# Causal triangle by matmul in the first two blocks, a new queue model in the planner, and a new order of the whole kernel

## The chip, the cores and the metric

The kernel runs on one core of one Trainium2 chip. A core has five engines with a queue each, which take their instructions strictly in the order in which the program gives them: TensorE (PE, matmuls; its weight loads are listed as PEld), VectorE (DVE), ScalarE (ACT), GpSimd (POOL) and SyncE (SP). DMA transfers are issued from two of them: from SP, whose descriptors the hardware makes, and from POOL, where software makes them; a transfer from POOL can convert f32 to bf16 on its way. Both kinds run on the same 16 DMA engines. The metric is the device time of one execution in microseconds; less is better.

## What is computed

The reference is causal attention with a choice of key chunks, followed by a two-layer network with a softplus between the layers. Cut to what matters:

```python
# q, k, v: (4, 8, 768, 64) f32; w_in: (512, 2048), w_out: (2048, 512)
k_min, k_max = k_chunks.min(3), k_chunks.max(3)          # chunks of 32 keys
ub = sum(maximum(q * k_min, q * k_max), axis=-1)          # bound per query and chunk
ub = where(causal, ub, -1e9)
top_chunks = argsort(ub)[..., -6:]                        # 6 chunks per query
scores = q @ k.T / 8
scores = where(selected & (pos_q >= pos_k), scores, -1e9)
attn = softmax(scores)
x = attn @ v                                              # (3072, 512)
h = x @ w_in
out = softplus(h) @ w_out                                 # f32
```

## The kernel before

The 3072 rows are 12 blocks of 256 queries: 4 batches with 3 blocks each. For each block n the kernel loads k, q and v, prepares them (k and q turned so that the head dimension lies on the partitions, the minima and maxima of the key chunks, the positive and negative part of q), computes the bounds with matmuls ("ub"), finds the sixth largest with DVE, and writes the resulting mask as extra rows below q, so that the score matmul adds the mask itself. These extra rows meet rows of ones and zeros per chunk (`ohb`, made by POOL and copied by SP into `KA` and `KB`, names "ohk"). For each of the 4 pairs of heads follow the scores ("s", lines 687 and 688), the exponential on ACT ("ex", line 695), the product with v ("av", line 717), the division by the sum ("nm", lines 727 and 728, into a buffer of the pool `osb`), and the turning of the result into `x`: by PE ("oT", line 743) in blocks 0 to 2 and 11, by a DMA transpose from SP ("xD") in the others. Then come the layers: "h" (line 791: 8 groups of 8 matmuls per block), two exponentials ("e", line 796) and a logarithm ("ln", line 801), and "y" (line 816), copied out and stored.

In the block on the diagonal, keys after the query must not count. Inside a 128 by 128 tile this triangle is cut out by POOL, after the exponential, with an affine select on `pt` ("af", line 705), and the product with v waits for it.

The first loads differ from the later ones. k and q of block 0 are loaded as f32 by SP (`load_pairs`, line 352) into `xp` and cast by ACT; everything else is loaded and cast by POOL (`load`, line 339; weights at 376 and 383). k and q are turned by PE in blocks 0 to 2 (line 471), by DMA transposes from block 3 on.

The order of the instructions is not written by hand. `make_plan` lists operations with a cost per engine, with what they need, and with a due time; `Plan.run` places them one after the other on a model of the engines and of two DMA queues, and takes the operation that is due first among those that can start soonest (within a tolerance `tol` per engine). Buffers come from pools whose sizes stand in `PAR["sizes"]`. The due times come from `PAR` (`a`, `prep`, `hlag` and others). `keep_awake` (line 852) then puts matmuls of zeros into the gaps that the plan leaves on PE in the first 45 us. The result is a fixed order on each engine; on the chip an instruction waits only for what it needs and for what stands ahead of it in its queue. In particular `rel`, the earliest time of an operation, is read only here:

```python
    def data_at(self, o, e):
        if e not in o.at:
            t = o.rel
            for d in o.deps + o.gate:
```

Block 3's loads and some copies on SP have a real dependency on the last piece of w_out (`gate`).

## Time and profile before

| | us |
|---|---|
| median of 3 runs | 267.46 (266.27 to 268.2) |
| the profiled execution | 266.59 |
| its span, first to last instruction | 264.8 |
| zero matmuls on PE (line 852), 243 of them | 22.7 |
| selects of the triangle on POOL (line 705), 96 of them | 39.5 |
| granted clock of TensorE, mean | 0.994 |

Busy time of an engine is what its instructions took; the page gives it as a share of the span. In the lists of instructions a row has the start and the time in us, the engine, the line, the operation, output and inputs, the count of like instructions in a row, and in square brackets how long the engine had been idle before and what ended that. "SPq" and "POOL ... DMA" rows are the issue of a transfer, not the transfer itself. Views by stage give the length of the stage, busy time and count (x) of each engine, the granted clock, the mean number of DMA packets at work per DMA engine, and GB/s.

### The profile page before, as it was taken

What the parts mean: (1) busy time and instruction counts of PE and PEld (TensorE: products, weight loads), DVE (VectorE), ACT (ScalarE), POOL (GpSimd) and SP (SyncE); (2) the same over time, 40 slices, a digit from 0 to 9 for tenths busy, and PEclk for the clock granted to TensorE, in tenths of its full rate; (3) what the DMA queues carried; (4) which work ended last, traced back from release to release, by engine and by line L of the source; (5) the groups of instructions that cost most, each with busy time, mean ns of one, the idle gap of its engine ahead of it and who ended that gap; (6) DMA issues with size and microseconds to landing.
All of it is one profiled execution on the core that took longest, in us unless ns stands there. A gap on an engine that the chain in (4) does not pass through costs nothing.

```text
span 264.8 us, 7039 instructions
## 1 busy us (share of the span) xinstructions
PE 255.0 (96%) x2750; PEld 197.2 (74%) x2779; DVE 142.5 (54%) x500; ACT 211.0 (80%) x372; POOL 110.8 (42%) x193
## 2 busy tenths in 40 slices
PE   8698999999999999999999999999999999999995
PEld 8698898768775677788678864777888756887744
DVE  6589961019789667447634596584582164221012
ACT  3589999988687879999687992699997885999900
POOL 8927878798318520543990263401110211310000
PEclk9799999999999999999999999999999999999999
DMA  7996999999999984699699969624440123001022
GB/s 162 161 189 90 181 196 231 155 139 190 149 136 173 132 119 89 115 129 100 73 173 150 117 88 174 173 54 120 45 82 0 42 72 99 10 2 42 0 79 79
DMA packets 114719, 29.87 MB, mean 113 GB/s; under 512 B 104544, under 2 KB 111712, under 8 KB 114688
## 3 DMA queue, kind: packets, MB, share of 16 engines
q0 software_dynamic: 74944, 13.11, 66.5%
q1 hardware_dynamic: 39744, 16.33, 33.0%
q8 instruction: 21, 0.34, 0.6%
q14 instruction: 10, 0.08, 0.1%
HBM read 27.26 MB, written 6.29 MB: 127 GB/s over the span
## 4 chain that ended last, share of the span: by engine, by line
PE 86%; DMA 5%; DVE 3%; ACT 3%; issue 1%; POOL 0%; DVEq 0%; POOLq 0%
PE ph L791 30%; PE py L816 17%; PE pt L816 9%; PE po L717 7%; PE ps L687 5%; PE py L852 4%; PE ps L688 4%; DMA io<-in_k_dram 3%; DMA x<-osb 3%; PE pt L687 2%; PE pt L688 1%; PE pt L570 1%; ACT g L801 1%; PE ph L816 1%; ACT e L796 1%
## 5 line engine op out<-in xcount | busy, mean ns | idle before, releaser
L791 PE MATMUL ph<-x,w_in_sb 128*128 128x256 bf16 x768 | 91.8, 272 | 0.0
L705 POOL TENSOR_SCALAR_AFFINE_SELECT pt<-pt 128x256 bf16<-128x256 bf16 x96 | 39.5, 419 | 112.6 <-ACT pt L695 112.1
L791 PEld LDWEIGHTS <-w_in_sb 128*128 128x128 bf16 x768 | 73.6, 98 | 11.5 <-DMA w_in_sb<-in_moe_w_in_dram 0.5
L695 ACT ACTIVATE pt<-ps 128x512 bf16<-128x512 f32 (+1 forms) x134 | 69.9, 564 | 9.4 <-PE ps L688 8.8
L796 ACT ACTIVATE e<-ph 128x512 f32<-128x512 f32 x96 | 56.3, 606 | 12.5 <-PE ph L791 11.8
L816 PEld LDWEIGHTS <-g 128*128 128x128 bf16 x400 | 37.4, 98 | 31.4 <-ACT g L801 0.5
L816 PE MATMUL py<-w_out_sb,g 128*128 128x512 bf16 x231 | 57.8, 379 | 1.5 <-ACT ysb L258 0.2
L801 ACT ACTIVATE g<-e 128x1024 bf16<-128x1024 f32 x48 | 51.1, 1072 | 1.0
L695 ACT ACTIVATE pt<-pt 128x512 bf16<-128x512 f32 (+1 forms) x58 | 32.4, 584 | 0.6 <-PE pt L688 0.6
L717 PEld LDWEIGHTS <-pt 128*128 128x128 bf16 x672 | 26.8, 97 | 5.1 <-issue 0.6
L259 DVE COPY ysb<-py 128x512 f32<-128x512 f32 x12 | 8.3, 691 | 36.9 <-PE py L816 36.9
L717 PE MATMUL po<-v,pt 128*128 128x65 bf16 x610 | 26.4, 193 | 0.3 <-DVE osb L728 0.3
L816 PE MATMUL pt<-w_out_sb,g 128*128 128x512 bf16 x108 | 26.2, 379 | 0.2
L727 DVE RECIPROCAL rec<-po 128x4 f32<-128x4 f32 x43 | 7.6, 178 | 34.9 <-PE po L717 34.6
L490 DVE TENSOR_REDUCE kx<-kT 128x32 bf16<-128x1024 bf16 x18 | 21.0, 1209 | 8.9 <-DMA kT<-io 8.9
L852 PE MATMUL py<-zero 128*128 128x128 bf16 x243 | 22.7, 245 | 1.1 <-DVE zero L268 1.1
L339 POOL DMA_DIRECT2D v<-in_v_dram x24 | 21.6, 905 | 3.8 <-DMA io<-in_q_dram 1.5
L339 POOL DMA_DIRECT2D io<-in_k_dram x22 | 20.0, 910 | 5.7 <-DMA w_in_sb<-in_moe_w_in_dram 2.2
L339 POOL DMA_DIRECT2D io<-in_q_dram x22 | 19.9, 910 | 0.7 <-PE ph L791 0.6
L728 DVE TENSOR_TENSOR osb<-po,rec 128x256 bf16<-128x256 f32 x43 | 18.2, 424 | 2.7 <-DMA x<-osb 1.3
L852 PEld LDWEIGHTS <-zero 128*128 128x128 bf16 x243 | 18.3, 111 | 1.3 <-DVE zero L268 1.1
L687 PE MATMUL ps<-qa,ka 96*128 96x256 bf16 x71 | 18.3, 273 | 0.7 <-DVE qa L259 0.7
(99 smaller groups left out, 302.5 us busy)
## 6 DMA issues: line engine op xcount, KB each, us to landing
out_dram<-ysb SPq DMA_DIRECT2D x23, 256.0 KB, 2.4
v<-in_v_dram POOLq DMA_DIRECT2D x24, 128.0 KB, 7.6
io<-in_k_dram POOLq DMA_DIRECT2D x22, 128.0 KB, 7.2
io<-in_q_dram POOLq DMA_DIRECT2D x22, 128.0 KB, 7.1
w_out_sb<-in_moe_w_out_dram POOLq DMA_DIRECT2D x4, 512.0 KB, 8.0
w_in_sb<-in_moe_w_in_dram POOLq DMA_DIRECT2D x4, 512.0 KB, 9.6
xp<-in_k_dram SPq DMA_DIRECT2D x2, 256.0 KB, 3.2
xp<-in_q_dram SPq DMA_DIRECT2D x2, 256.0 KB, 6.3
```

What stands on the lines that cost most here:

```text
L339: lambda e, t=t: nc.gpsimd.dma_start(out=into(nm, n, t), in_=rows(nm, n, t)),
L490: nc.vector.tensor_reduce(kx.ap[:, :, j].rearrange("d p (t c) -> d t p c", t=NT), kT.ap.rearrange("d p x -> d (p x)").rearrange("d (t p c ...
L687: nc.tensor.matmul(sp.ap[:, 0:QB], kk[0:nr, p, j * 128:(j + 1) * 128], qq, start=True, stop=True)
L695: lambda e, sp=sp, pt=pt, h=h, j=j, w=w: nc.scalar.activation(pt.ap[:, h, j:j + 2].rearrange("k j c -> k (j c)")[:, 0:w], sp.ap[:, 0:w], A ...
L705: nc.gpsimd.affine_select(out=d, in_=d, compare_op=ALU.is_ge, fill=0.0, base=0, channel_multiplier=-1, pattern=[[0, 2], [1, 128]])
L717: nc.tensor.matmul(o[:, u, h], pt.ap[:, h, j, c0:c0 + 128], T.V[i][:, j, 2 * p + h, :], start=(j == 0), stop=(j == t0 + u))
L728: nc.vector.tensor_tensor(osb.ap[0], o[:, :, :, 0:D], osb.ap[1].to_broadcast([128, NT, 2, D]), op=ALU.mult)
L791: nc.tensor.matmul(o[:, j], T.w_in[:, dt, ft * 128:(ft + 1) * 128], x.ap[:, dt], start=(dt == 0), stop=(dt == KDM - 1))
L796: lambda e, hb=hb, eb=eb, f2=f2: nc.scalar.activation(eb.ap[:, f2 * 512:(f2 + 1) * 512], hb.ap, ACT.Exp),
L801: lambda e, eb=eb, g=g, f4=f4: nc.scalar.activation(g.ap[:, f4 * 4:(f4 + 1) * 4].rearrange("f j c -> f (j c)"), eb.ap, ACT.Ln, bias=1.0),
L816: nc.tensor.matmul(yb.ap[:, 0:c1 - c0], g.ap[:, f, u * 128:(u + 1) * 128], T.w_out[:, f, c0:c1], start=(f == 0), stop=(f == KFF - 1))
L852: z.fn = lambda e: T.nc.tensor.matmul(T.pools["y"].homes[0][:, 0:128], T.zero, T.zero, start=True, stop=True)
```

## The change

The triangle of blocks 0 and 1 (`tri=2`) is no longer selected by POOL. Two more matmuls per last score group add a tile `T.tri` (0 where the key counts, -240000 where it doesn't) through the identity, before the exponential; the 16 selects of these blocks go. The zero matmuls may be 512 columns wide. The planner gets a new model of the two DMA queues (`Rings`): packets alternate between the two, a transfer that starts late is held back, at most 7 software transfers are out at once, and landing times change by kind (`land`, `packet`, `pen`). The software loads of blocks 0 to 2 get `rel=3300`. All due times are new, a table `tweak` adds an offset to the due time of about 170 names of operations, `tol` of POOL goes from 2358 to 9819 and of ACT from 0 to 150, `alt` (the handicap of an operation's second engine) from 636 to 48. The pools io, osb and e shrink from 8, 4 and 4 buffers to 6, 3 and 2. Options `both` and `l0 >= 3` are added and not used.

```diff
+class Rings:
+    def __init__(self):
+        self.t, self.q, self.on = 0.0, {"POOL": [], "SP": []}, {"POOL": False, "SP": False}
+        self.slots = []
...
+    def add(self, o, now):
+        self.run(max(now, self.t), [])
+        e = "POOL" if o.eng == "POOL" else "SP"
+        if e == "POOL":
+            if len(self.slots) >= 7:
+                o.end = max(o.end, self.slots[-7].done - self.slots[-7].land + 200)
+            self.slots.append(o)
...
+        for o in topo:
+            o.due += 1e3 * par["tweak"].get(o.name, 0.0)
...
-    tol={"PE": 0, "ACT": 0, "DVE": 0, "POOL": 2358, "SP": 0},
-    alt=636,
-    a=(-46.8, -33.92, -31.03, -0.05, 17.1, 24.77, 54.71, 88.7, 133.12, 175.62, 173.66, 255.42, 297.45, 469.8),
-    sizes=dict(s=2, h=2, y=1, o=1, t=2, xf=2, xp=4, kT=2, io=8, kx=2, q=2, pn=2, ub=2, pt=4, osb=4, x=4, g=2, e=4, ysb=4, mT=2),
+    tol={"PE": 0, "ACT": 150, "DVE": 0, "POOL": 9819, "SP": 0},
+    alt=48,
+    a=(-73.83, -47.43, -47.0, -44.3, 27.28, 71.21, 103.27, 111.52, 147.33, 256.72, 285.03, 350.27, 490.15, 633.52),
+    sizes=dict(s=2, h=2, y=1, o=1, t=2, xf=2, xp=4, kT=2, io=6, kx=2, q=2, pn=2, ub=2, pt=4, osb=3, x=4, g=2, e=2, ysb=4, mT=2),
...
+    tri_ = []
+    if par["tri"]:
+        t0_ = P.op("tri0", [("DVE", 100)], lambda e: nc.vector.memset(T.tri, 0.0), key=2000)
+        tri_ = [P.op("tri", [("POOL", 430)], lambda e: nc.gpsimd.affine_select(
+            out=T.tri, in_=T.tri, compare_op=ALU.is_ge, fill=NEG, base=0, channel_multiplier=-1, pattern=[[1, 128]]), [t0_], key=8000), ident]
...
-                     gate=gate, key=key, rel=key - 2000 if n > 2 else 0.0, dma=950 if n < 3 else 2050, packet=32.0, **new)
+                     gate=gate, key=key, rel=key - 2000 if n > 2 else 3300.0 if par["l0"] == 1 else 0.0, dma=850, packet=13.3, land=SKEW if n < 4 else 900.0, **new)
...
-                        nc.tensor.matmul(sp.ap[:, 0:QB], kk[0:nr, p, j * 128:(j + 1) * 128], qq, start=True, stop=True)
-                        nc.tensor.matmul(sp.ap[:, QB:w], kk[0:nr, p, (j + 1) * 128:(j + 2) * 128],
-                                         qq[:, 1] if last else qq, start=True, stop=True)
+                        add = last and tri
+                        for c0, c1, x in ((0, QB, qq), (QB, w, qq[:, 1] if last else qq)):
+                            jj = j + c0 // QB
+                            nc.tensor.matmul(sp.ap[:, c0:c1], kk[0:nr, p, jj * 128:(jj + 1) * 128], x, start=True, stop=not add)
+                            if add:
+                                nc.tensor.matmul(sp.ap[:, c0:c0 + 128], T.ident, T.tri, start=False, stop=True)
...
-                    if last:
+                    if last and not tri:
...
-        while True:
-            c = 107 if t < 1e3 * par["awake"][2] else mm(128)
...
+        for w in (512, 128):
+            while True:
+                c = w / 1.2 if t < 1e3 * par["awake"][2] else mm(w)
...
-    T.zero = sb.tile([128, 128], BF16, name="zero")
+    T.zero = sb.tile([128, 512], BF16, name="zero")
+    T.tri = sb.tile([128, 128], BF16, name="tri")
```

In `tweak` the names at issue below read `"w_out1": 70.83`, `"w_out0": -10.19`, `"w_in0": -1.54`, `"w_in1": 8.48`, `"oh": 19.6`, `"tri": -1.15`; the pieces of w_in and of w_out keep their order among themselves.

More of the change, by code (lines that the diff above doesn't have):

```diff
@@ L65 @@
 class Op:
     __slots__ = ("name", "alts", "fn", "deps", "gate", "after", "succ", "alloc", "touch", "key",
-                 "rel", "packet", "port", "due", "wait", "eng", "start", "end", "done", "dma", "n", "at", "inst")
+                 "rel", "packet", "port", "land", "pen", "due", "wait", "eng", "start", "end", "done", "dma", "n", "at", "inst")
 class Plan:
@@ L837, in keep_awake @@
 def keep_awake(T, order, par):
-    fill, free = [], 1e3 * par["awake"][0]
+    fill, free = [], max(1e3 * par["awake"][0], 140 + next(o.end for o in order if o.name == "zero"))
     for o in order:
```

204 lines of the change are left out of this document (141 added, 63 removed).

## The prediction

> **What bounds the kernel now.** I read the page first, then the busy time of each engine by stage, then the zero matmuls of line 852 by the same stages, and last the timeline of the first 44 us.
>
> ```profile
> span 264.8 us, 7039 instructions
> PE 255.0 (96%) x2750; PEld 197.2 (74%) x2779; DVE 142.5 (54%) x500; ACT 211.0 (80%) x372; POOL 110.8 (42%) x193
> ```
>
> PE is busy 96% of the span and no other engine is above 80%. But a part of PE's time is filler, so the average must be split into stages.
>
> ```profile
> core 0: us, PE busy (x) PEld busy (x) DVE busy (x) ACT busy (x) POOL busy (x), PEclk, DMA share, GB/s
> 0.00:18.00 18.00, 14.69 (x187) 14.13 (x188) 12.10 (x38) 10.22 (x15) 14.30 (x28) 0.91 1.57 167
> 18.00:28.00 10.00, 9.21 (x161) 8.43 (x160) 9.54 (x35) 9.47 (x16) 6.56 (x13) 1.00 0.86 123
> 28.00:36.00 8.00, 7.58 (x131) 6.68 (x129) 7.50 (x34) 7.78 (x17) 6.46 (x13) 1.00 1.34 184
> 36.00:44.00 8.00, 8.00 (x103) 7.27 (x102) 2.59 (x10) 7.35 (x15) 6.80 (x11) 1.00 1.22 220
> 44.00:261.20 217.20, 215.19 (x2175) 160.65 (x2202) 109.88 (x383) 176.17 (x312) 76.65 (x131) 1.00 0.95 102
> 261.20:264.80 3.60, 0.34 (x4) 0.06 (x1) 0.85 (x2) 0.00 (x0) 0.00 (x0) 1.00 0.21 73
> ```
>
> The zero matmuls alone, in the same stages:
>
> ```profile
> 0.00:18.00 18.00, 11.95 (x115) 10.19 (x115) 0.91 1.57 167
> 18.00:28.00 10.00, 6.48 (x87) 5.17 (x86) 1.00 0.86 123
> 28.00:36.00 8.00, 3.09 (x33) 2.19 (x33) 1.00 1.34 184
> 36.00:44.00 8.00, 1.21 (x10) 0.71 (x10) 1.00 1.22 220
> ```
>
> From 44 us to the last matmul PE is idle for 217.2 - 215.2 = 2.0 us and runs no zeros: that stretch holds real work from end to end, and the change takes none of it away. Up to 44 us PE spends 11.95 + 6.48 + 3.09 + 1.21 = 22.7 us on zeros and 3.31 + 0.79 + 0.42 = 4.5 us idle. Those 27 us (somewhat less, as the modelled ends overlap) are what a better start can win, and the tail of 3.6 us is untouched. Between 18 and 36 us both DVE (17.0 of 18) and ACT (17.3 of 18) are nearly full, so in there an earlier start helps by moving the whole block of work forward, not by squeezing it.
>
> What delays the start shows in the timeline up to the first score matmul.
>
> ```profile
> 0.81 1.00 SPq L352 DMA_DIRECT2D xp<-in_k_dram  x2
> 1.85 1.06 SPq L352 DMA_DIRECT2D xp<-in_q_dram  x2
> 2.08 1.90 POOL L339 DMA_DIRECT2D io<-in_k_dram  x2
> 3.84 0.62 ACT L258 CAST io<-xp 128x512 bf16<-128x512 f32 x1 [1.75 <-DMA xp<-in_k_dram]
> 4.72 0.62 ACT L258 CAST io<-xp 128x512 bf16<-128x512 f32 x1 [0.26 <-DMA xp<-in_k_dram]
> 7.67 0.62 ACT L258 CAST io<-xp 128x512 bf16<-128x512 f32 x1 [2.33 <-DMA xp<-in_q_dram]
> 9.50 0.62 PE L471 MATMUL ph<-ident,io 128*128 128x128 bf16 x8 [2.24 <-DMA io<-in_k_dram]
> 9.96 2.39 PE L852 MATMUL py<-zero 128*128 128x128 bf16 x23
> 10.16 0.59 ACT L258 COPY qt<-ph 128x512 bf16<-128x512 bf16 x1 [0.80 <-PE ph L471]
> 12.03 0.90 PEld L471 LDWEIGHTS <-io 128*128 128x128 bf16 x8
> 12.13 0.63 PE L471 MATMUL ph<-ident,io 128*128 128x128 bf16 x4
> 16.32 0.38 PE L471 MATMUL pt<-ident,io 128*128 128x128 bf16 x4
> 18.04 0.27 PE L687 MATMUL ps<-qa,ka 96*128 96x256 bf16 x1
> ```
>
> The two f32 loads of k arrive 0.88 us apart (3.84, 4.72). The first f32 load of q should follow at that pace, about 5.6, but ACT gets it at 7.67: POOL's software loads began at 2.08 and share the transfer time. Then PE waits 2.24 us for a software load of k, and in the same group of eight transposes stand the four of q, whose cast was ready at 7.67 + 0.62 = 8.29. PE takes its queue in order, so q of block 0 (copied out at 10.16) waited behind a k that is not needed yet. Last, the 23 zeros take 104 ns each, where the four transposes at 16.32 start (0.38 - 0.218) / 3 = 54 ns apart (0.218 being the mean of one, quoted below): PE ran them at half clock.
>
> ```profile
> 8.00:12.00 4.00, 2.50 (x30) 2.50 (x31) 2.00 (x6) 3.18 (x7) 3.86 (x8) 0.78 2.41 159
> 12.00:16.00 4.00, 4.00 (x75) 4.00 (x73) 2.51 (x12) 2.29 (x4) 3.17 (x6) 0.79 2.01 169
> 20.00:24.00 4.00, 3.31 (x68) 3.07 (x67) 3.88 (x11) 3.94 (x7) 3.79 (x9) 1.00 0.35 67
> ```
>
> The granted clock of 0.78 and 0.79 is that. The third row is the other loss: from 20 to 24 us the DMA engines are nearly unused (0.35 against 2.41).
>
> **The change, part by part.** The profiled execution took 266.59 us, 1.8 us outside its span; the median of the runs is 267.46, 0.87 above it. The sum is made from 266.59, and 0.87 added at the end.
>
> *Software loads behind the f32 ones, with a new queue model.* The release of 3.3 us exists in the planner only: no instruction waits for it, so POOL may still issue at 2.08. What does change is the order that the planner writes: it now believes that a software load lands later, so the transposes of k that stood before those of q will stand behind them. Lower bound of the gain: q's transposes move from behind the wait, about 9.72 (half of the group at 9.50 comes first), to 8.4, 1.3 us. Upper bound: q also lands at 5.6, its cast ends at 6.2 and its transposes run at 6.3, 3.4 us earlier. Below the lower bound lies zero, if another engine of the chain is late instead: ACT and DVE were busy 10.22 and 12.10 of the first 18 us, so they have 7.8 and 5.9 us to give. I take 2.0, nearer to the lower bound, because nothing enforces the hold. What moves with it: the loads of blocks 1 and 2, each followed by its casts and transposes, and the row copies on SP, which were issued at about 10 us behind four loads.
>
> *No idle gap, so no half clock.* If PE has filler or work instead of the 2.24 us gap, the 23 zeros cost 23 x 54 = 1.24 us instead of 2.39, and the eight transposes behind them 0.25 us less per four. That is 1.15 + 0.5 = 1.65 us at most, nothing at least (the gap moves elsewhere). I take 0.6, since part of it is inside the term above. The Trainium skill (TensorE: Matmul & The Clock Gate, Part 1) says that the clock is set per window of about 3.4 us from how busy PE was in it, in windows that run free of the kernel. The trace agrees: after the gap PE stays slow until about 13.4, and by that rule alone this term would be the full 1.65.
>
> *Triangle by matmul in blocks 0 and 1.* 16 selects leave POOL, and 32 matmuls of 128 columns with their weight loads join PE.
>
> ```profile
> L705 POOL TENSOR_SCALAR_AFFINE_SELECT pt<-pt x16: 396/408/579, 20.1 to 38.2; 128x256 bf16<-128x256 bf16 x16
>   ACT pt L695: 7.8, 7
> L743 PE MATMUL pt<-ident,osb 128*128 128x128 bf16 x32 | 4.1, 218 | 0.4 <-DVE qneg L549 0.4
> 20.07 0.78 POOL L705 TENSOR_SCALAR_AFFINE_SELECT pt<-pt 128x256 bf16<-128x256 bf16 x2 [4.76 <-ACT pt L695]
> 27.55 0.77 POOL L376 DMA_DIRECT2D w_in_sb<-in_moe_w_in_dram  x1
> 35.43 0.77 POOL L376 DMA_DIRECT2D w_in_sb<-in_moe_w_in_dram  x1 [0.21 <-issue]
> 36.06 1.03 PE L791 MATMUL ph<-x,w_in_sb 128*128 128x256 bf16 x8
> ```
>
> On PE: 32 x 54 ns = 1.7 us, covered by the 6.48 + 3.09 = 9.6 us of zeros between 18 and 36 us, so I cost it at nothing; without that cover it is 1.7. The Trainium skill (TensorE: Matmul & The Clock Gate, Back-to-back issue gap) gives 81 ns for each pair of weight load and matmul at 128 columns in a real stream. That would make 2.6 us; the transposes here start 54 ns apart, each with its own weight load, so the row decides.
>
> The change adds one wait: the score matmuls of blocks 0 and 1 need the triangle's own select on POOL, about 0.4 us, which stands in one queue with the loads. If it came after too many of them, all of PE's queue behind the first score would wait. These scores wait already for rows that POOL must select first, so I cost it at nothing; each load put ahead of it wrongly costs about 0.95 us (two at 2.08 took 1.90).
>
> On POOL: 16 x 0.408 = 6.5 us of work go, and with them 7.8 us in which POOL stood waiting for ACT's exponentials while loads stood behind it in the queue. The longest such wait, 4.76 us before 20.07, lies just ahead of the idle stretch of the DMA engines. The first piece of w_in was issued only at 27.55, the last at 35.43, and the first matmul on it started at 36.06. The table of tweaks delays w_out1 by 70.83 us of due time, and w_out2 and w_out3 must follow it, so less stands ahead of w_in. What an earlier w_in can save is the zeros and idle from 28 to 44 us: 3.09 + 1.21 + 0.42 = 4.7 us. It can't be all, since x of block 0 must be there too and comes through DVE and ACT, full until 36 us. I take half, 2.4; the bounds are 0 and 4.7.
>
> *Wide zeros.* 512 columns in one instruction are four times 104 or 54 ns: the same time. A zero that stands too long ahead of a ready matmul delays it by up to 0.4 us instead of 0.1. I take 0, with 0.5 either way.
>
> *Smaller pools, order anew.* io goes from 8 to 6 buffers, osb from 4 to 3, e from 4 to 2. Both exponentials and the logarithm that empty and fill e are on ACT, which takes them in order, so I cost that at 0. The io loads run tens of us ahead in the full stretch. osb is the doubtful one and is priced as a rival. In the full stretch the gain is at most the idle 2.0 us; I take 0.
>
> Sum: 266.59 - 2.0 - 0.6 - 2.4 = 261.6, and 262.5 against the median. Its own range runs from 260 to 264.7.
>
> **The rivals.**
>
> *The hold is only on paper (chance 0.19).* POOL issues at 2.08 as before, q lands at 7.67 again, and the new order, written for an earlier q, has ACT and PE wait for it in queue order. Then the first term is 1.3, the second 0, and w_in gains perhaps 0.7: 267.46 - 2.0 = 265.5. For it: the release is read by the planner alone. Against it: the triangle and the w_in order don't depend on it.
>
> *The full gain (0.15).* q arrives at 5.6 (3.4), the clock stays up (1.65) and w_in meets x early (4.7). The sum is 9.75 with some of it counted twice, so about 9: 258.5. For it: 27 us of PE time stand open. Against it: DVE and ACT are full from 18 to 36 us and lose little work.
>
> *osb as the new bound (0.18, slower).* With three buffers, the normalisation of one pair waits until the DMA transpose of the pair three before has landed, po stays occupied, and PE, which has no slack after 44 us, waits.
>
> ```profile
> L728 DVE TENSOR_TENSOR osb<-po,rec 128x256 bf16<-128x256 f32 x43 | 18.2, 424 | 2.7 <-DMA x<-osb 1.3
> x<-osb SPq DMA_TRANSPOSE x32, 2.7
> 87.22 7.05 DMA x<-osb
> ```
>
> For it: even with four buffers DVE once waited 1.3 us for such a landing, and one of them took 7.05 us on the chain of waits. Against it: the median is 2.7 us, less than three pairs take. If each of the 8 blocks with these transposes loses 1 us, 8 - 5 = 3 us are lost: 270.5. It decides from 0.6 us per block on, where it eats the 5 us of the start.
>
> **How the numbers follow.** The forecast has 0.48, the rivals 0.19, 0.15 and 0.18. A measurement of this kernel can tell about 1% from no change, that is 2.7 us: faster means below 264.8. Forecast and full gain lie there, 0.63; the paper rival lies within 1%, 0.19; osb is slower, 0.18. The range of 8 in 10 goes from 258, which cuts off half of the full gain (0.07), to 269, which leaves out the upper two thirds of osb (0.12).
>
> **What would show it.** In the profile after: the second pair of casts from xp should start well before 7.67; no wait of PE for a software load near 9 us, and a granted clock of 1.0 from 8 to 16 us; the first score before 16.5; the first matmul of line 791's counterpart before 32; fewer than 18 us of zeros; PE idle after that no more than 2 us. POOL's waits for ACT before 40 us should be gone. The forecast is wrong if q is cast at 7.6 or later and the first score stays at 18, or if PE shows waits for osb, po or io in the full stretch.

## The result and the profile after

The changed kernel took 268.73 us (median of 20 runs, 266.57 to 270.84), the kernel before beside it 265.85 us (20 runs, 263.88 to 268.2). The ratio is 1.0107, with a 95% interval of 1.0077 to 1.0137: slower by a little over 1%, where 262.5 us and a gain were forecast. Some executions fall into a slower state; the ratios here and below leave these out, the medians in us do not. The profiled execution took 268.23 us.

The page of the changed kernel has these two lines for the two of before:

```profile
span 266.5 us, 6768 instructions
PE 250.9 (94%) x2600; PEld 186.5 (70%) x2635; DVE 132.8 (50%) x484; ACT 218.7 (82%) x387; POOL 104.7 (39%) x180
```

PE is less busy and the span is longer, so PE stands idle where it did not before. The view by stage says where (start and end of the stage, its length, then busy time of each engine):

```profile
0.00:18.00 18.00, 14.80 (x137) 8.77 (x140) 14.49 (x44) 13.29 (x22) 16.10 (x34) 1.00 1.35 157
18.00:28.00 10.00, 8.94 (x121) 6.76 (x120) 8.07 (x32) 8.27 (x20) 7.42 (x12) 1.00 1.64 167
28.00:36.00 8.00, 7.95 (x136) 7.16 (x135) 6.85 (x33) 7.35 (x15) 3.88 (x5) 1.00 1.24 206
36.00:44.00 8.00, 7.46 (x78) 6.21 (x76) 2.03 (x6) 6.80 (x13) 0.81 (x2) 1.00 1.50 192
44.00:263.00 219.00, 211.41 (x2142) 157.51 (x2170) 101.32 (x371) 182.31 (x321) 76.44 (x129) 1.00 0.85 100
```

Its zero matmuls alone, in the first three stages (there are none after 28 us):

```profile
0.00:18.00 18.00, 10.84 (x44) 4.46 (x46) 1.00 1.35 157
18.00:28.00 10.00, 3.49 (x19) 1.75 (x21) 1.00 1.64 167
28.00:36.00 8.00, 0.00 (x0) 0.00 (x0) 1.00 1.24 206
```

In this profile the start came out as hoped: 14.3 us of zeros instead of 22.7, the clock at 1.00, no dead stretch of the DMA engines between 18 and 28 us (1.64 against 0.86). The full stretch did not: PE is idle for 219.0 - 211.4 = 7.6 us there, against 2.0 before. The lines of the timeline that answer to those of before:

```profile
3.85 0.62 ACT L332 CAST io<-xp 128x512 bf16<-128x512 f32 x1 [1.76 <-DMA xp<-in_q_dram]
4.74 0.62 ACT L332 CAST io<-xp 128x512 bf16<-128x512 f32 x1 [0.27 <-DMA xp<-in_k_dram]
5.77 0.62 ACT L332 CAST io<-xp 128x512 bf16<-128x512 f32 x1 [0.41 <-DMA xp<-in_q_dram]
15.41 0.28 PE L799 MATMUL ps<-qa,ka 96*128 96x256 bf16 x1 [1.41 <-DMA ka<-ohb]
20.82 2.32 POOL L469 DMA_DIRECT2D w_in_sb<-in_moe_w_in_dram  x3
27.64 1.03 PE L903 MATMUL ph<-x,w_in_sb 128*128 128x256 bf16 x8
```

Three casts are done by 6.4 us, the first score comes at 15.41 (18.04 before), the pieces of w_in are issued by 23.1 (35.43), and the first matmul on them is at 27.64 (36.06).

To compare orders that differ, I count work instead of busy time: the number of weight loads of each kind up to a moment, each at its distance in a full stretch (16 h matmuls in 1.75 us are 109.2 ns each, y 215.7, product with v 30.2, scores 95.9 on average, bounds 25, transposes and triangle 55.6). The whole kernel before is 238.0 us of such work, the triangle adds 1.8. (Of these, 3.4 us are too much in every row, because 32 of the last y matmuls are half as wide; the differences between rows are not touched.) What is left of the time up to a moment is **lost PE time**.

| lost PE time, us | by 44 us | by 95 us | by 140 us | to the end | span |
|---|---|---|---|---|---|
| before | 25.0 | 26.1 | 26.2 | 26.8 | 264.8 |
| before, second profile | 24.2 | 24.8 | 25.0 | 25.6 | 263.6 |
| before with the triangle (1.8 us more work) | 21.1 | 21.5 | 21.6 | 23.4 | 263.2 |
| changed | 18.9 | 23.9 | 26.3 | 26.7 | 266.5 |
| changed, narrow zeros, beside the control | 18.5 | 22.2 | 22.6 | 23.4 | 263.2 |
| changed, 19 zeros fewer | 18.1 | 23.7 | 24.2 | 25.1 | 264.9 |
| changed, narrow zeros, 19 more | 18.8 | 22.7 | 25.7 | 26.4 | 266.2 |

The rows below the first and the fourth belong to the experiments. Between these two profiles, then, 6.1 us were won at the start (part of that is the run and not the change; the section on why the prediction was wrong works it out), 3.9 given back from 44 to 95 us and 2.3 from 95 to 140, and 1.8 us of triangle came on top: the 1.7 us between the spans. The experiments ask why those two stretches gave it back.

### The profile page after: what moved, and what is told of

It reads as the page before. It is cut to its first block, busy times and chain, and to the rows that moved or that the text cites. A ratio compares the mean times of both kernels' runs of the same rounds, so it can differ in the third digit from the quotient of the medians.

```text
span 266.5 us, 6768 instructions
## 1 busy us (share of the span) xinstructions
PE 250.9 (94%) x2600; PEld 186.5 (70%) x2635; DVE 132.8 (50%) x484; ACT 218.7 (82%) x387; POOL 104.7 (39%) x180
## 4 chain that ended last, share of the span: by engine, by line
PE 72%; DMA 12%; DVE 5%; ACT 5%; POOL 3%; issue 2%; POOLq 0%; SPq 0%; DVEq 0%
PE ph L903 25%; PE py L928 17%; PE pt L928 8%; PE ps L799 8%; PE po L829 5%; DMA qt<-io 4%; PE pt L799 3%; DMA kT<-io 3%; DMA io<-in_k_dram 2%; DMA ka<-ohb 2%; ACT pt L807 2%; DMA mT<-mraw 2%; PE pt L678 1%; PE ph L928 1%; POOL io L418 1%
## 5 line engine op out<-in xcount | busy, mean ns | idle before, releaser
L903 PE MATMUL ph<-x,w_in_sb 128*128 128x256 bf16 x768 | 94.5, 272 | 0.7 <-DMA x<-osb 0.7
L817 POOL TENSOR_SCALAR_AFFINE_SELECT pt<-pt 128x256 bf16<-128x256 bf16 x80 | 32.3, 421 | 119.7 <-ACT pt L807 119.5
L807 ACT ACTIVATE pt<-ps 128x512 bf16<-128x512 f32 (+1 forms) x139 | 71.5, 554 | 7.2 <-PE ps L799 5.1
L928 PE MATMUL py<-w_out_sb,g 128*128 128x512 bf16 x244 | 63.4, 379 | 1.5
L807 ACT ACTIVATE pt<-pt 128x512 bf16<-128x512 f32 (+1 forms) x53 | 29.6, 575 | 1.1 <-PE pt L799 1.1
L829 PEld LDWEIGHTS <-pt 128*128 128x128 bf16 x672 | 26.4, 97 | 5.4 <-issue 0.8
L799 PE MATMUL ps<-qa,ka 96*128 96x256 bf16 (+1 forms) x138 | 23.8, 257 | 2.6 <-DMA ka<-ohb 1.4
L799 PE MATMUL ps<-qt,kb 128*128 128x256 bf16 (+1 forms) x140 | 23.7, 259 | 1.5 <-ACT pt L807 1.5
L799 PEld LDWEIGHTS <-ka 96*128 96x128 bf16 x192 | 17.4, 98 | 8.5 <-DMA ka<-ohb 1.6
L928 PE MATMUL pt<-w_out_sb,g 128*128 128x512 bf16 x93 | 22.5, 379 | 0.2
L799 PEld LDWEIGHTS <-kb 128*128 128x128 bf16 x192 | 16.7, 97 | 6.7 <-issue 1.8
```

The source lines that it names most:

```text
L799: nc.tensor.matmul(sp.ap[:, c0:c1], kk[0:nr, p, jj * 128:(jj + 1) * 128], x, start=True, stop=not add)
L807: lambda e, sp=sp, pt=pt, h=h, j=j, w=w: nc.scalar.activation(pt.ap[:, h, j:j + 2].rearrange("k j c -> k (j c)")[:, 0:w], sp.ap[:, 0:w], A ...
L817: nc.gpsimd.affine_select(out=d, in_=d, compare_op=ALU.is_ge, fill=0.0, base=0, channel_multiplier=-1, pattern=[[0, 2], [1, 128]])
L829: nc.tensor.matmul(o[:, u, h], pt.ap[:, h, j, c0:c0 + 128], T.V[i][:, j, 2 * p + h, :], start=(j == 0), stop=(j == t0 + u))
L903: nc.tensor.matmul(o[:, j], T.w_in[:, dt, ft * 128:(ft + 1) * 128], x.ap[:, dt], start=(dt == 0), stop=(dt == KDM - 1))
L928: nc.tensor.matmul(yb.ap[:, 0:c1 - c0], g.ap[:, f, u * 128:(u + 1) * 128], T.w_out[:, f, c0:c1], start=(f == 0), stop=(f == KFF - 1))
```

## The experiments

### What PE waited for at 66 us

The chain of waits of the changed kernel (start, us, what) around the largest loss:

```profile
48.85 0.35 POOL pt L817
49.20 5.33 DMA io<-in_k_dram
...
54.59 7.63 DMA kT<-io
62.22 0.02 issue
62.24 2.36 DVE kx L598 x2
...
65.31 0.20 DVE rec L839
...
65.53 0.43 DVE osb L840
...
66.01 0.28 PE pt L855 x2
```

The last row stands in the timeline with what PE waited for:

```profile
66.01 0.28 PE L855 MATMUL pt<-ident,osb 128*128 128x128 bf16 x2 [3.10 <-DVE osb L840]
```

Read backwards: PE's transposes waited 3.1 us for `osb`; osb stood on DVE behind the chunk minima of block 3 (`kx`), which wait for a DMA transpose of k; that one was issued at 54.59 and took 7.63 us, because its k had been loaded only at 49.20, behind selects of block 2 in POOL's queue. The kernel before has the same step, seen in its timeline:

```profile
49.48 1.35 SPq L475 DMA_TRANSPOSE kT<-io  x1
59.67 2.34 DVE L490 TENSOR_REDUCE kx<-kT 128x32 bf16<-128x1024 bf16 x2
```

There the transpose is issued at 49.48, takes 8.5 us, and DVE comes for it at 59.67 with no wait at all. So the wait that names osb is not a shortage of osb buffers. Theory A was that a few steps of the new order stand wrong and can be put right; theory B that from about 56 us PE has used up what the transfers could deliver.

**DVE's steps of block 3 behind those of block 2.** All edits of this kind move planned instructions after the planner has run; `place` sets their place in the order, in us.

```diff
+    place(named(order, "kx3") + named(order, "kn3") + named(order, "bd3"), 58.3)
```

> The changed kernel with one edit in DVE's queue: the reduces of k of block 3 (and the copy of their result) stand behind the last division of block 2 instead of ahead of it. Theory A (DVE takes its queue in order, stood 3.78 us at these reduces until the turned k of block 3 landed at 62.24, and the division behind them held PE for 3.10 us): that idle time of PE goes, the ratio to the kernel before falls by about 2.4 us of 266 (from 1.011 to about 1.002), since the bounds of block 3 then wait for the late k by themselves for some 0.7 us. Theory B (from 56 us on PE has simply used up what the transfers have delivered, so the loss is owed anyway): PE idles the same 3 us a little later, before the scores of block 3, and the ratio stays within 0.003 of 1.011.

Measured: 268.46 us, ratio 1.0109 (1.0066 to 1.0153). The stall at 66 us is gone: from 56 to 68 us 0.4 us are lost instead of 3.3. But 1.7 are lost from 68 to 80 instead of 0.1, 1.6 from 80 to 95 and 2.5 from 125 to 140. The stall moved on.

**Buffers.** The changed kernel's order with the pool sizes of before (3 pools, the same instructions).

```diff
+    for kind, size in (("io", 8), ("osb", 4), ("e", 4)):
+        pool = T.pools[kind]
...
```

> The changed kernel in its own order on every engine, with the three pools at their sizes of before (io 8, osb 4, e 4 buffers, given out in turn). The rival of the prediction (three osb buffers hold the division and through it PE): the waits of DVE for landings of x (0.2 and 0.5 us near 91 us) and some idle time of PE go, 1 us or more in all, ratio below 1.007. Theory A: no change, ratio 1.008 to 1.014, since the waits on osb in the trace add up to less than 1 us and the one idle time of PE of 3.1 us has another cause.

Measured: 269.19 us, 1.0142 (1.009 to 1.0195), and PE waits for osb as before:

```profile
65.11 0.28 PE L855 MATMUL pt<-ident,osb 128*128 128x128 bf16 x2 [3.15 <-DVE osb L840]
```

The smaller pools cost nothing that can be seen.

**Block 3 exchanged with block 4.** The new order loads k of block 4 ahead of block 3. Here they change places, and block 3 loses its dependency on w_out.

```diff
+    for x in ("ld k%d.0", "ld k%d.1", "ld q%d.0", "kD%d", "kx%d", "kn%d", "bd%d"):
+        swap(named(order, x % 3)[0], named(order, x % 4)[0])
...
+    for x in ("ld k3.0", "ld k3.1", "ld q3.0", "ld q3.1"):
+        named(order, x)[0].gate = []
```

> The changed kernel with blocks 3 and 4 exchanged in the early queues: k and q of block 3 are loaded where those of block 4 were (28.5 to 35 us) and no longer wait for the last piece of w_out; k of block 4 takes the places of block 3, its reduces behind block 3's bounds. Theory A (block 3 came late because its loads alone waited for w_out, while block 4's passed them): the turned k of block 3 lands before 53 instead of at 62.24, PE's idle time from 56 to 68 us (3.3 us of lost work) goes, most of the next loss too, and the time falls by 3 to 5 us: ratio 0.993 to 1.000. Theory B (the transfers can't deliver more by then): PE runs dry over block 4 instead, ratio 1.005 to 1.011.

Measured: 269.87 us, 1.0172 (1.0113 to 1.0231). Nothing is lost from 56 to 68, but 6.4 us from 68 to 80, where DVE waits for transposes of q (2.18 us at 68.79, after 2.87 at 64.51). The granted clock was 0.93 from 44 to 95 us in this profile, so a part of that loss is the clock's.

**Other loads held while k of block 3 is turned.**

```diff
+    late = [named(order, x)[0] for x in ("ld v3.0", "ld v3.1", "ld q4.1", "ld v4.0", "ld v4.1")]
+    place(late, 54.0)
+    late[0].gate = named(order, "kD3")
```

> The changed kernel with five software loads (both of v of block 3, the second of q of block 4, both of v of block 4) held back until the turned k of block 3 has landed; they stand behind the triangle selects of block 2 on POOL. Theory C (that turning took 7.63 us from issue to landing, against 3.1 at the least, because it shared the DMA engines with these loads): it lands after some 4 us, at about 58.5, DVE goes on 3.5 us earlier and PE's 3.10 us of idle time go: 2 to 3 us less, ratio near 1.001. If sharing isn't the cause, the landing stays at 7 us or more and the ratio at 1.011 or above, since the held loads come later.

Measured: 271.34 us, 1.0221 (1.0172 to 1.027). The transpose of k of block 3, issued at 54.11 with hardly a software packet beside it, landed after 3.0 us instead of 7.6 (some 4 were expected). Nothing was lost from 56 to 68 us, but 7.3 us from 68 to 80: DVE waits 6.14 us for q of block 4, which was among the held (and the granted clock was 0.97 from 44 to 95 us). So the loads beside that transpose are what made it slow, and they could not wait either.

**Five loads of blocks 3 and 4 at 34 us, ahead of the selects of block 2,** alone and together with the first edit.

```diff
+    ops = [named(order, x)[0] for x in ("ld k3.0", "ld k3.1", "ld q3.0", "ld q3.1", "ld q4.1")]
+    for o in ops:
+        o.gate = []
+    place(ops, 34.0)
```

> The changed kernel with five loads (k and q of block 3, the second of q of block 4) moved ahead in POOL's queue, to before the first triangle select of block 2, and without their wait for w_out; everything else in its place. Theory A (block 3 is late because these loads stood behind the selects, which wait for ACT, and behind w_out's landing): k of block 3 is issued before 40 instead of at 47.95, its turned form lands near 55 instead of 62.24, the turned q of block 4 near 60 instead of 68, PE's lost 3.3 us from 56 to 68 go and don't come back: ratio 0.995 to 1.003. Theory B (the DMA engines, over 90% busy from 7 to 86 us, deliver no sooner, or the loss moves on to the next block): ratio 1.008 to 1.014.

> The same with the reduces of block 3 behind the last division of block 2 on DVE (the edit of the first experiment). Theory A: both stalls of PE before 95 us are gone; 4 to 6 us less than the changed kernel, ratio 0.988 to 0.998, faster than the kernel before. Theory B: as without it, within 0.004.

Measured: 268.27 us, 1.0069 (1.0029 to 1.0108), and with both edits 269.24 us, 1.0131 (1.0076 to 1.0185). From 44 to 95 us the first loses 5.3 us, the second 4.0, the changed kernel 5.0.

**A longer software load in the planner,** 1150 ns for blocks 3 and up instead of 850, and all planned again.

```diff
-dma=850, packet=13.3, ...
+dma=850 if n < 3 else 1150, packet=13.3, ...
```

> The changed kernel, planned anew with one number of the model changed: a software load of blocks 3 and later holds its queue for 1150 ns instead of 850 (the kernel before had 2050). In the trace of the changed kernel 29 loads were issued in the 29 us from 47.95 to 77 with the queue never empty. Theory A (the plan believed these loads too fast, so the engines' queues hold steps of blocks 3 and 4 ahead of work that was ready): the new order puts that work first, PE's lost work between 56 and 140 us falls from 6.8 to about 3, ratio 0.997 to 1.004. Theory B: no less lost work, ratio above 1.007. Its due times are not tuned to the new number, which can cost some of the gain.

Measured: 270.57 us, 1.0196 (1.0158 to 1.0235). The loss from 56 to 68 us is gone, and 4.8 us come from 80 to 95.

Six repairs, no gain beyond what one of them may have (0.4%, intervals overlapping). That speaks against theory A in its simple form. The next runs speak against theory B, for a part of the loss.

### The triangle and the transposes, each by itself

**The changed kernel without its 32 triangle matmuls,** so that blocks 0 and 1 see later keys.

```diff
-                            if add:
-                                nc.tensor.matmul(sp.ap[:, c0:c0 + 128], T.ident, T.tri, start=False, stop=True)
```

> The changed kernel without the 32 matmuls that add the triangle in blocks 0 and 1: keys after the query then count in these blocks, and that part of the computation is left out. All other instructions and their order stay. Theory A (these matmuls stand in a stretch in which PE has zeros or waits anyway, and their 1.8 us fill no gap that is lost later): 1 to 1.8 us less if PE is full from 28 us on, none if what is gained early is lost at 62 us again. Theory B: nothing is gained (ratio within 0.003 of 1.011), since PE waits for block 3 at the same time anyway.

Measured: 266.25 us, 1.0046 (1.0012 to 1.008). I first read this as the price of the triangle, 1.6 us paid in full. The last pair of runs below takes most of that reading back.

**The transposes of k of block 2 behind those of q of block 0,** in the kernel before.

```diff
+    k2, q0 = named(order, "kT2"), named(order, "qT0")
+    place(k2[:1], 6.97)
+    place(k2[1:], 8.78)
```

> The kernel before with one step moved on PE: the two groups of transposes of k of block 2 are queued behind those of q of block 0; no load, no other instruction moves. Theory A (a start gain stays gained where the order behind it is not drawn anew): the start shortens by up to 2.0 us, no half clock in the second slice, and the time falls by 1 to 2 us, ratio 0.992 to 0.996. Theory B (from about 56 us on the transfers set the pace, whatever the start): lost PE time falls by 1 to 2 us up to 28 us and is back by 140 us; ratio 0.998 to 1.002.

**The triangle alone,** in the kernel before: 16 selects out of POOL's queue, 32 matmuls in.

```diff
+    for o in named(order, "s0") + named(order, "s1"):
+        o.end += 110
+    return [o for o in sorted(...) if o.name not in ("af0", "af1")]
...
+                            if add:
+                                nc.tensor.matmul(sp.ap[:, c0:c0 + 128], T.ident, T.tri, start=False, stop=True)
```

> The kernel before with the triangle alone: the 16 selects of blocks 0 and 1 are left out of POOL's queue, the 32 triangle matmuls are added behind the scores, the order of all else is kept. The forecast's step (the matmuls are covered by the zeros, and POOL, free of its waits, issues w_in earlier): ratio 0.990 to 0.998, the first h matmul some 2 us earlier. The reading from the run without triangle matmuls (their 1.7 us are paid whatever POOL gains): ratio 1.004 to 1.007, with w_in earlier all the same.

**Both together.**

> Both edits together in the kernel before: the triangle by matmul and the transposes of k of block 2 behind those of q of block 0. If start gains are kept where the order is not drawn anew, the sum of both: under theory A 0.985 to 0.994; under theory B, with the triangle paid and the start gain given back, 1.004 to 1.007.

Measured: 1.0024 (0.9994 to 1.0053), 1.0003 (0.9967 to 1.0039) and 0.9995 (0.996 to 1.0031); no difference can be told. The lost PE time of the triangle alone says more: 21.1 us by 44 us, where the kernel before has 25.0 (24.2 in a second profile, below), 21.5 by 95 and 21.6 by 140. (With both edits it is 21.5 by 44 us, so the two do not add.) A start that is 3 to 4 us better (against profiles with a dip of the clock, which this one lacks) keeps that through the whole busy stretch; 1.8 us of it go only between 140 us and the end (23.4), and the triangle's own 1.8 take the rest. Its view by stage:

```profile
44.00:95.00 51.00, 50.84 (x536) 36.92 (x534) 31.61 (x114) 42.90 (x79) 31.23 (x48) 1.00 1.78 147
95.00:140.00 45.00, 45.00 (x480) 35.20 (x478) 22.84 (x83) 40.21 (x70) 22.65 (x34) 1.00 1.11 116
```

PE is idle 0.16 us from 44 to 95 us. The same rows of the changed kernel:

```profile
44.00:95.00 51.00, 46.14 (x470) 33.36 (x476) 31.42 (x96) 40.91 (x74) 32.14 (x46) 1.00 1.68 164
95.00:140.00 45.00, 43.13 (x484) 34.20 (x490) 25.53 (x107) 40.88 (x73) 12.79 (x25) 1.00 0.63 84
```

4.86 and 1.87 us. So theory B falls for about half of the loss: by 95 us the old order had lost 21.5 us, the new one 23.9, and these 2.4 us belong to the new order of the stretch, since the transfers could be made to deliver in time. Whether they could also have carried the 18.9 us with which the changed kernel enters the stretch, no run shows.

### The zeros, which should not matter

**The changed kernel with 128-wide zeros,** its order kept.

```diff
-        for w in (512, 128):
+        for w in (128,):
```

> The changed kernel with its zero matmuls 128 wide again, its order kept. The forecast costed the wide zeros at nothing, plus or minus 0.5 us: ratio to the kernel before as the changed kernel has it, 1.008 to 1.013, the clock 1.00 in the first 16 us. If the wide zeros delay real work behind them, the time falls by 0.5 us or more: 1.005 to 1.008. If narrow zeros let the clock drop, it rises above 1.013.

Measured: 265.95 us, 1.0029 (0.9993 to 1.0065), 0.8% below the changed kernel. Up to 44 us the two lose the same (18.6 and 18.9), so the zeros did not delay the work around them; the difference comes later, most of it from 125 to 140 us, 100 us behind the last zero. Since it ran on another chip than the changed kernel, both were run side by side, with two more:

> The changed kernel as it is, run beside the next one on one chip. If the zeros' width is what the run with narrow zeros showed, this stays at 1.008 to 1.013 while that one stays near 1.003; if the chip or the hour made that difference, both come out alike, within 0.004 of each other.

> The changed kernel with 128-wide zeros, beside the changed kernel on the same chip. Theory W (a wide zero that has begun holds back the real matmul that becomes ready behind it, and moves the times at which transfers are issued): 0.5 to 1.0% below the control. Theory C (chance of the chip): within 0.4% of it.

The change's loop alone, in the kernel before:

```diff
+        for w in (512, 128):
...
+                c = w / 1.2 if t < 1e3 * par["awake"][2] else mm(w)
```

> The kernel before with the wide zeros alone, order kept. Theory W: 1.003 or more, with a longer lost time before 44 us. Theory C: 0.997 to 1.003.

And the kernel before once more, for a second profile:

> The kernel before as it is, one profile more. Its profiled run above had a granted clock of 0.89 in the first 16 us, and a second profile shows whether that belongs to the kernel. If the dip is in it by rule, the span is 264 to 265 and the clock in 8 to 12 us about 0.5; if not, the span is 262 to 263 and what the forecast counted for the dip (0.6 us) was never there in most runs.

Measured: the changed kernel 268.15 us, 1.0079 (1.0044 to 1.0114); with narrow zeros 266.29, 1.0024 (0.9993 to 1.0056); the wide zeros in the kernel before 263.86, 0.9944 (0.9899 to 0.9988); the second profile of the kernel before has a span of 263.6 us. Side by side on one chip the two differ again the same way, by 0.55%, though the intervals just overlap; so the chip alone did not make the difference. Nor does the width as such: in the kernel before, wide zeros make it faster, which neither theory had, and that version is the fastest of all that were run. Its lost time is 22.2 us by 44 us and 24.3 at the end (25.6 in the second profile of before). Why is not settled; the clock may be part of it, since five of its six runs had a mean granted clock of 0.998 or more.

The granted clock itself came out otherwise than the forecast had it. Both profiles of the kernel before show it low between 8 and 12 us (0.78 and 0.57), but of its 24 runs in this group 14 have a mean clock of 0.998 or more (median 264.8 us) and 10 a lower one (266.1 without one of 268.4). The changed kernel does the same: 9 of its first 20 runs are below 0.998, and the control's profile reads

```profile
8.00:12.00 4.00, 4.00 (x27) 2.46 (x26) 2.16 (x4) 2.95 (x6) 3.68 (x8) 0.64 2.00 128
```

where the changed kernel's first profile has 1.00 throughout.

### An instruction fetch inside a transpose

What differs between wide and narrow zeros 100 us later? The same transpose of the mask of block 6, on SP and at its reader on DVE, in the timeline of the changed kernel:

```profile
109.24 1.19 SPq L744 DMA_TRANSPOSE mT<-mraw  x1
113.66 0.76 DVE L333 COPY qa<-mT 32x512 bf16<-32x512 bf16 x2 [4.45 <-DMA mT<-mraw]
125.73 0.43 DVE L659 TENSOR_SCALAR qpos<-qt 128x1024 bf16<-128x1024 bf16 x1 [2.55 <-DMA qt<-io]
135.17 0.43 DVE L659 TENSOR_SCALAR qpos<-qt 128x1024 bf16<-128x1024 bf16 x1 [2.65 <-DMA qt<-io]
```

and with narrow zeros:

```profile
107.50 1.19 SPq L744 DMA_TRANSPOSE mT<-mraw  x1
110.11 0.58 DVE L333 COPY qa<-mT 32x512 bf16<-32x512 bf16 x2 [2.65 <-DMA mT<-mraw]
121.59 0.43 DVE L659 TENSOR_SCALAR qpos<-qt 128x1024 bf16<-128x1024 bf16 x1 [0.48 <-DMA qt<-io]
131.59 0.43 DVE L659 TENSOR_SCALAR qpos<-qt 128x1024 bf16<-128x1024 bf16 x1 [1.12 <-DMA qt<-io]
```

From issue to landing these are 4.4 us against 2.6 for one instruction at the same place of the same order. The DMA queues of the changed kernel from 110.5 to 111.5 us (packets, MB, share; above 100% where packets overlap):

```profile
q1 hardware_dynamic: 464, 0.11, 217.4%
q8 instruction: 1, 0.02, 5.7%
```

and with narrow zeros from 109.8 to 111.0, when the transpose is over:

```profile
q8 instruction: 1, 0.02, 5.5%
```

One packet of instructions was fetched in the middle of the transpose in the one kernel and behind it in the other. Queue q8 carries 20 such packets in the changed kernel, 0.33 MB, about 16 KB each; PE runs 2635 weight loads and as many matmuls, so there is a packet for about every 260 of PE's instructions. The Trainium skill (Runtime: NRT & Kernel Launch, Instruction fetch mechanics) gives 256 instructions for a block of 16 KiB, and the trace agrees. Then the number of zeros decides where all later fetches fall. The narrow version has 176 zeros instead of 67, which is 218 instructions more, or 38 short of one packet. Two kernels test this: 38 instructions less with wide zeros, 38 more with narrow ones.

```diff
+                small += w == 128
-                fill.append(z)
+                if w == 512 or small <= 11:
+                    fill.append(z)
```

> The changed kernel with its wide zeros, but without the last 19 of its 128-wide ones (38 PE instructions less before 28 us). Theory F: what the narrow zeros changed is not their width but where PE's 16 KB instruction fetches fall. They come about every 256 PE instructions; in the two profiles of the changed kernel one of them (at 111.0) fell into the transpose of the mask issued at 109.24 and 109.32, which took 4.4 and 4.1 us instead of 2.5, and the stall of 1.7 and 4.4 us from 125 to 140 us followed. Narrow zeros put 218 instructions more ahead, less than a whole fetch by 38. So 38 less bring the same phase: fetch 1.5 to 2 us later against that transpose, transpose 2.4 to 2.8 us, lost time from 125 to 140 us under 0.6 us, ratio 1.001 to 1.006, like the narrow one. Theory W (the width): nothing of this, ratio 1.008 to 1.011.

```diff
+                if t > 12500 and more:
+                    more -= 1
...
+                    z.fn = x.fn = lambda e: T.nc.tensor.matmul(T.pools["y"].homes[0][:, 0:64], T.zero[:, 0:128],
+                                                               T.zero[:, 0:64], start=True, stop=True)
+                    fill.append(x)
```

> The changed kernel with narrow zeros and 19 of them split in two of 64 columns (38 PE instructions more). Theory F: the fetch falls into that transpose again as in the changed kernel: transpose 3.8 to 4.6 us, 1.5 to 3 us lost from 125 to 140 us, ratio 1.006 to 1.011. Theory W: like the narrow one, 1.001 to 1.005.

Wide zeros, 19 fewer, by stage and in the timeline:

```profile
95.00:140.00 45.00, 44.63 (x515) 36.02 (x520) 26.20 (x112) 41.81 (x75) 12.87 (x25) 1.00 0.62 87
```

```profile
108.99 1.19 SPq L744 DMA_TRANSPOSE mT<-mraw  x1
111.55 0.58 DVE L333 COPY qa<-mT 32x512 bf16<-32x512 bf16 x2 [2.59 <-DMA mT<-mraw]
```

Narrow zeros, 19 more:

```profile
95.00:140.00 45.00, 42.54 (x480) 33.66 (x485) 24.76 (x105) 40.12 (x71) 12.37 (x24) 1.00 0.64 82
```

```profile
107.99 1.19 SPq L744 DMA_TRANSPOSE mT<-mraw  x1
112.16 1.02 DVE L333 COPY qa<-mT 32x512 bf16<-32x512 bf16 x2 [4.19 <-DMA mT<-mraw]
```

Both came out as theory F has it: a transpose of 2.5 us and PE idle for 0.37 us with the fetch at 112.1, when the transpose is over; 4.1 us and 2.46 us idle with the fetch at 109.9, inside it. (The fetch moved by about 1 us against the transpose, where 1.5 to 2 was expected.) The times are 266.43 us, 1.0042 (1.0015 to 1.0069) and 267.98 us, 1.0071 (1.0038 to 1.0103). The first is outside what theory W has; the intervals of the two overlap, so the times alone would not prove it. The ratios go the forecast way by 0.3%, as did those of the pair before them by 0.55%. Of the 14 profiles of the changed kernel and of versions with its planner, ten have the slow transpose (3.8 to 4.4 us) and PE idle 1.1 to 2.5 us from 95 to 140 us (3.1 in the control, whose clock was 0.97 there); the four with a fast one (2.5 to 2.6 us) have 0.07 to 0.37. Those four are the narrow zeros (two runs), the wide ones less 19, and the run without triangle matmuls, which has 64 PE instructions fewer. In one of the ten, the order planned again, software loads ran beside that transpose as well. With the triangle or without, then, kernels that miss the collision stand at 1.0024 to 1.0046: no price of the triangle can be seen.

The way from there to 140 us leads over a second collision. The late mask by itself costs PE little: 0.16 us at 116.06. The next fetch of the changed kernel, at 122.9, falls into a transpose of q; with narrow zeros none falls into it (first row the changed kernel, second row narrow zeros):

```profile
120.50 1.23 SPq L583 DMA_TRANSPOSE qt<-io  x1
118.44 1.23 SPq L583 DMA_TRANSPOSE qt<-io  x1
```

DVE has what they bring at 125.73 and 121.59, in the rows above: this transpose took 5.2 us instead of 3.1 (4.8 to 5.4 in the ten profiles, 3.1 to 3.3 in the four). DVE takes its instructions in order and starts the next rec and osb late, with them go the transposes of x, behind which SP issues the next q, and PE waits for both in the changed kernel:

```profile
131.01 1.58 PE L903 MATMUL ph<-x,w_in_sb 128*128 128x256 bf16 x13 [0.67 <-DMA x<-osb]
135.66 0.19 PE L678 MATMUL pt<-bd,qpos 128*128 128x32 bf16 x1 [0.46 <-DVE qpos L659]
```

With narrow zeros PE has no such wait from 109 to 141 us. The two collisions come together in every profile, so the runs don't say what each costs.

## Why the prediction was wrong

**The start was forecast in its direction and not in its size.** The forecast put 5.0 us there (2.0 + 0.6 + 2.4). Lost PE time by 44 us fell by 6.1, or 4.3 with the triangle's work counted against it, which looks near. But both profiles of the kernel before have a low clock at the start, and the first profile of the changed kernel has none. With the dip on both sides it is 25.0 and 24.2 against 20.0 in the control: 4.2 to 5.0, and 2.4 to 3.2 after the triangle. Without it on either side, the old order with wide zeros has 22.2 and the changed kernel 18.9: 3.3, and 1.5 after the triangle. In the same two profiles of before the first q came late too: ACT cast it at 7.67 and 7.24, and the first score came at 18.04 and 17.36. Three versions that keep the old loads and have no dip (transposes of q first, triangle alone, wide zeros) have 6.2 to 6.6 and 15.1 to 15.4, and the changed kernel 5.77 and 15.41. So most of the earlier first score belongs to the run that was profiled, and the terms of 2.0 and 0.6 were read from that run. What clearly came is w_in: the first h is at 27.64 (29.03 with the dip), in the old order at 33.36 with wide zeros and no dip, and at 35.38 and 36.06 with the dip. The software loads did stay behind: POOL's first one is at 3.02, though nothing waits for the release, because the triangle's own select and its wait for DVE stand ahead of it. So the rival of the hold on paper did not come about. w_in came at 17.3 to 23.1 as reasoned, and POOL's waits for ACT before 40 us are gone.

**Two of its terms don't hold alone.** The transposes of k behind those of q, made in the kernel before, save 1.3 to 2.1 us by 44 us against the two profiles of before and no time; that profile has no dip, and the dip is worth 1.1 us by 44 us between the two profiles of the changed kernel, so 0.2 to 1.0 us are left for the term of 2.0. And the half clock, 0.6 us, was read from one profile: it is in some runs of either kernel and not in others, 1.3 us apart in the kernel before, so the change could not take it out. The Trainium skill (TensorE: Matmul & The Clock Gate, Part 1) says that the windows run free of the kernel, so that the same kernel meets them differently from run to run. The runs agree with that: 14 of 24 without the dip, 10 with it. The forecast quoted this page and still counted the dip as a property of the kernel.

**The triangle at nothing held.** Alone in the kernel before it gives 1.0003 (0.9967 to 1.0039). Its 1.8 us of work are paid, and the better start of that version pays them back.

**The failed step is "Smaller pools, order anew",** which says: "In the full stretch the gain is at most the idle 2.0 us; I take 0." That bounds the gain and forgets the loss. An order with 2 us of idle time in 217 has nowhere to go but down when all of it is drawn anew, and it went down: PE's idle time in the full stretch grew from 2.0 to 7.6 us, of which 4.86 lie between 44 and 95 us and 1.87 between 95 and 140. The first part comes with the new order of blocks 3 and 4: the transpose of k of block 3 is issued 5 us later than before, with 7.6 us to go beside a full queue of software loads, and 3.0 us when these were held. Repairs of single places moved the loss and did not remove it. The second part is the fetches that fell into two transposes, worth 0.55% and 0.3% in two pairs of runs; without them the change stands at 1.0024 to 1.0042, not to be told from no change in two of three.

**The slower rival had the right sign with the wrong mechanism.** That the measured 268.73 us lies inside the range that was given (258 to 269) is luck, since the upper end of the range rests on this rival. The profile does show PE waiting 3.1 us for osb, which the forecast had named as its sign of failure. But with four buffers again the wait stayed at 3.15 us; osb was late because it stood behind a waiting instruction on DVE. "Wide zeros: 0, with 0.5 either way" was right for what it argued, the time of the zeros and the delay of work near them, and missed that their number moves all later fetches.

What stays open: which steps of the new order cost the 2.4 to 4.9 us lost from 44 to 95 us, why wide zeros make the kernel before faster by 0.6%, and what each of the two collisions costs.

## What to carry to other kernels

When a change draws a whole order anew, price the stretch that was already full as a risk, not as a zero: list the transfers with the longest way there (here the DMA transposes of k and q) and how long before their use each is issued. Before a dip of the clock is priced, take a second profile: here the first score came anywhere from 15.1 to 18.0 us with the same loads in the same order. A wait names the last thing that was late; look at what stands ahead of it in its own queue before counting buffers. And when an edit far away changes time at a place whose instructions are the same, compare the instruction queue's packets at that place; shifting the instruction count by a handful is a cheap test, and it should be made before a difference of half a per cent is put down to the edit.

## What the runs showed of the hardware

- An instruction fetch of about 16 KB that falls into a DMA transpose can lengthen it: that of the mask of block 6 from 2.5 to 2.6 us to 3.8 to 4.4 us (four and ten profiles). It is not a matter of this one place: in the 20 profiles 121 transposes of a mask ran with no software packet beside them. The 60 that met no instruction packet took 2.4 to 2.6 us; the 39 in which a packet of q8 began, more than 0.2 us before the landing, took 2.8 to 4.4 us. In the changed kernel 43 small packets trickled in between 111.5 and 114 us, behind the fetch. That the fetch holds up one of the 16 DMA engines is my reading; the views do not show single engines. The same section of the Trainium skill's page Runtime: NRT & Kernel Launch calls the cost of crossing a block mostly hidden. For the engine that fetches nothing here speaks against it, since no wait of PE is put down to a fetch; a transfer that meets the fetch does pay.
- A DMA transpose depends on its company. In the changed kernel, from 58 to 100 us and from 125 to 140 us (queue with packets, MB and share; issue with median us to landing):

```profile
q0 software_dynamic: 20837, 2.63, 98.7%
...
kT<-io SPq DMA_TRANSPOSE x3, 7.0
```

```profile
q0 software_dynamic: 2080, 0.26, 27.5%
...
kT<-io SPq DMA_TRANSPOSE x1, 3.1
```

  The same kind of transpose takes 7.0 us (median of three) beside a full software queue; the one issued at 124.59, with no software packet beside it until it landed, took 3.1, and that of k of block 3 fell from 7.6 to 3.0 us when the loads beside it were held.
- Runs of the kernel before with and without the low clock lie 1.3 us apart (266.1 and 264.8), a quarter of the 5.0 us that the change was to win.
